# Weight loads of 512 columns, four gates at the start of tile 0, and a reordered head in an attention and SwiGLU kernel

## The chip, the cores and the metric

The kernel runs on one core of a Trainium2 chip. Its time is the device time of one execution in microseconds (us), and what is given for a kernel is the median of several executions. One further execution was recorded by the hardware profiler, and all durations below are read from that one. The engines are called as in the profile: PE (matrix products; PEld are its weight loads), DVE, ACT, POOL and SP. POOL and SP appear here almost only as the engines that issue DMA transfers.

## The reference

Attention over 4 batches of 8 heads, 768 positions and 64 channels, with 8 global keys, a causal window of 96 and a distance bias, and after it a gated feed-forward block on 3072 tokens of width 512 (hidden width 1536):

```python
scores = scale * (q @ k.T)                                  # scale = 1/8
keep = (key < 8) | ((query - key >= 0) & (query - key < 96))
dist = where(global and not local, 96, abs(query - key))
a = softmax(where(keep, scores - slope[head] * dist, -1e9))
x = (a @ v) laid out as [3072 tokens, 512]
g = x @ w_gate
out = (g * sigmoid(g) * (x @ w_val)) @ w_out
```

## The kernel before

The 3072 tokens are cut into eight tiles of 384, two for each batch (its halves). The hidden width is cut into twelve blocks f of 128. For each tile t and block f, PE makes a gate and a value (`products`, line 538): four matmuls each, one for every 128 of the 512 input channels c, from the weights `wg` and `wv` and the tile's transposed input `xT`. ACT takes a tanh of the gate (`th`, line 558), DVE makes `sl` from it and the gate (line 560), and DVE multiplies value and `sl` into `hT` (line 564). `out_part` (line 568) adds three blocks of the output product (`ops`, weights `wo`) at a time, four parts for 128 tokens.

Attention lies between these products, written by hand into the order. The heads go in pairs hp = 0 to 3. Batch 0 is done in halves. For a half of a pair, `turn_half` (line 293) transposes keys and queries on PE (`trs`), `copy_half` (line 303) copies them out of PSUM into `kT` and `qT`, `bias` (line 334) writes the distance bias into two PSUM banks by matmuls with `slopeI` and `dist`, `scores_half` (line 345) adds the key and query products to it and issues the exponentials on ACT (line 361). `Quad` then sums two pairs: denominators (`den`) and numerators (`num`), and DVE scales the numerators into `xT` (a transpose on line 449, a reciprocal, a transpose on line 455, two products on line 497).

The order in time around the change is as follows. At the start 16 fill matmuls on constants run on PE (`fill`, line 609) while the first keys and queries of pair 0 come in as float32 over SP (`k32`, `q32`) and are cast on DVE and ACT (lines 632 and 633). The other loads go over POOL's queue, which casts on the way; eight semaphores go round among them, so an issue waits until the eighth one before it has landed. The head (lines 628 to 675) makes half 0 of batch 0. Then gates and values of blocks 0 and 1 of tile 0 are made in channel order as `xT` comes in (lines 677 to 682), and the table `half1` (line 762) puts half 1 of batch 0 between the blocks of tile 0: `trh` is the transposes of two pairs, `sch` the biases and scores of one pair, `va` the denominators and numerators of two pairs. `stretches` (line 769) lists tiles, blocks and how many output parts follow each block; for tile 1 its blocks 0 to 3 have 1, 0, 1, 0 parts.

PSUM has eight banks here: a0 to a3, which `bank()` gives out in turn; x0 to x2, which `spare()` gives out in turn (from block 9 on and up to block 2 of tile 1, seven banks go round there); and o0, for outputs and for the fill matmuls. In the head the banks are named one by one.

The weights are loaded by `load_w` (line 209) for a range of blocks: for each half of the channels one transfer of `wg` and one of `wv`, cast from float32 to float16. It is called for blocks 0 to 1, 2 to 3, 4 to 7 and 8 to 11, with the loads of half 1's keys and queries (`load_half(1, ...)`) and of the values of attention (`load_v_rest`) between them; then come `wo` in four quarters and the next batch. The values of the global keys (`vG32`) come in over SP, are cast into `vG` on ACT (line 635), and two SP transfers copy them to where the numerators read them (`copy_globals(0)` on line 636, and line 637 into `vCut`).

Of the kernel before, what the change touches and what calls it, by code (L numbers as in the profile page):

```python
# [37 lines left out]
def kernel(  # L38
# [12 lines left out]
    nc = tc.nc  # L51
# [157 lines left out]
    def load_w(f0, f1):  # L209
        a, z = 128 * f0, 128 * f1  # L210
        for g in range(2):
            for w, src in ((wg, moe_w_gate), (wv, moe_w_val)):
                nc.gpsimd.dma_start(  # L213
                    out=w[:, 2 * g:2 * g + 2, a:z],
                    in_=src[256 * g:256 * g + 256, a:z].rearrange("(p s) f -> p s f", s=2))
# [46 lines left out]
    class Pair:  # L262
        def __init__(self, b, hp):
            self.b, self.hp = b, hp
            self.at = {}

# [26 lines left out]
        def turn_half(self, half, tr):  # L293
            hp = self.hp
            trq, trk = tr
            for st, dst in ((k16, trk), (q16, trq)):
# [6 lines left out]
        def copy_half(self, half, tr, k_eng, q_eng):  # L303
            trq, trk = tr
# [21 lines left out]
            else:  # L326
                part(3, 4, cut * J2, KC, 0)
                part(4, 6, 0, KC, pc - cut)
                part(6, 7, 0, S - 6 * KC, 3 * pc - cut)
            q_eng(  # L330
# [221 lines left out]
    def gate_or_val(t, f, which, c0=0):  # L552
# [3 lines left out]
        if which == 0:  # L556
            th = sb2.tile([128, TB], FP32, name="th", tag="th")
            nc.scalar.activation(out=th, in_=dst[:, 0:TB], func=AF.Tanh, scale=0.5)  # L558
            sl = sb2.tile([128, TB], FP32, name="sl", tag="sl")
            nc.vector.scalar_tensor_tensor(  # L560
                out=sl, in0=th, scalar=1.0, in1=dst[:, 0:TB], op0=AluOp.add, op1=AluOp.mult)
            gv["sl"] = sl
        else:
            nc.vector.tensor_mul(hTs[t][:, f, :], dst[:, 0:TB], gv["sl"])  # L564
# [50 lines left out]
    def p_bias(hp, which, *tags):  # L615
        pairs[0, hp].sc = pairs[0, hp].bias(0, which, [single("sc", t) for t in tags])

    def p_sc(hp, which, *tags):
        if tags:
            p_bias(hp, which, *tags)  # L620
        pairs[0, hp].scores_half(0, which, pairs[0, hp].sc)

    def p_tr(hp, kt, qt, q_eng):
        tr = [single("trs", t, FP16)[:, 0:TB] for t in (qt, kt)]
# [4 lines left out]
    fill(16)  # L629
    for h in range(4):  # L630
        make_slope(nc.scalar.mul, h)
    A(out=q16[:, 0, 0:2], in_=q32)
    V(out=k16[:, 0, 0:2], in_=k32)
    p_tr(0, "x0", "x1", A)
    A(out=vG[:, 0], in_=vG32)
    copy_globals(0)
    nc.sync.dma_start(out=vCut[0:NG], in_=vG[:, 0])
    for h in range(4, 8):
        make_slope(nc.vector.tensor_scalar_mul, h)
    load_w(0, 2)  # L640
    load_half(1, 0, 4)
    load_w(2, 4)
    load_half(1, 4, 8)
    load_w(4, 8)
    for c in range(3, NCH):
        load_v_rest(0, c)
    load_w(8, 12)
# [10 lines left out]
    p_bias(0, 0, "a0", "a1")  # L658
    p_tr(1, "x2", "o0", V)
    p_sc(0, 0)  # L660
    p_sc(0, 1, "a2", "a3")
    p_sc(1, 0, "x0", "x1")
    p_tr(2, "a0", "a1", V)
    p_sc(1, 1, "x2", "o0")
    p_tr(3, "a2", "a3", A)
    p_sc(2, 0, "a0", "a1")
    quads[0, 0].denominators(single("den", "x0"))
    p_sc(2, 1, "a2", "a3")
    p_sc(3, 0, "a0", "a1")
    for side, tag in enumerate(("x1", "x2")):  # L670
        quads[0, 0].numerators(side, single("num", tag))
    p_sc(3, 1, "a2", "a3")
    quads[0, 1].denominators(single("den", "o0"))
    for side, tag in enumerate(("x0", "x1")):
# [209 lines left out]
```

## Time and profile before

| what | value |
|---|---|
| median of 6 runs | 244.03 us (243.04 to 244.69) |
| the profiled execution's own time | 243.98 us |
| its span, first to last instruction | 242.2 us |
| matmuls of gates on line 547 | 376, 0.327 us each as drawn |
| matmuls of outputs on line 576 | 276, 0.379 us each as drawn |
| tanh of a gate, ACT, line 558 | 94, 0.496 us each |
| `sl`, DVE, line 560 | 94, 0.551 us each |
| POOL issue of a weight load, line 213 | 16, 0.71 us each |
| `wg` loads of 128 KB, issue to landing | 4, median 4.9 us |
| `wg` loads of 256 KB, issue to landing | 4, median 7.7 us |
| `wo` loads of 384 KB, issue to landing | 4, median 10.4 us |
| granted TensorE clock, whole span | 1.000 |

The span is shorter than the execution's time by 1.8 us, which lies around it. A row of the timeline gives start, length, engine, line, operation, what it writes and reads, and how many of it are merged; in brackets stands the idle time of the engine before it and what ended it. Matmuls are drawn from issue to end, and follow each other more closely than their drawn length: the distance of starts is what one costs. The chain of work that ended last is followed back from the last instruction: at each step to what released it. A row of the windows view gives a stretch, its length, the busy time of PE, PEld, DVE, ACT and POOL with counts of instructions, the granted clock, and the share and rate of the DMA engines.

### The profile page before, as it was taken

How to read it: one execution, taken by the hardware profiler on the slowest of the kernel's cores; microseconds unless marked ns; L12 is line 12 of the kernel's file. 1: busy time of each engine (PE TensorE's matmuls, PEld its weight loads, DVE VectorE, ACT ScalarE, POOL GpSimd, SP SyncE). 2: the span in 40 equal slices, each digit the busy share in tenths (PEclk: the TensorE clock that was granted, in tenths of full speed). 3: DMA queues.
4: the chain of work that ended last, by engine and by line, in shares of the span. 5: the costliest groups of instructions: out<-in, count | busy, mean ns of one | idle time of the engine just before them, and what ended most of it. 6: DMA issues, size and time to landing. Idle time of an engine off the chain costs nothing.

```text
span 242.2 us, 6053 instructions
## 1 busy us (share of the span) xinstructions
PE 235.0 (97%) x2428; PEld 135.5 (56%) x2428; DVE 166.1 (69%) x355; ACT 129.1 (53%) x294; POOL 96.6 (40%) x117
## 2 busy tenths in 40 slices
PE   7899899999999999999999999999999999999994
PEld 4455466566565556555565556555565556555543
DVE  5675749878797768767786658767786558655530
ACT  5738476787864564365455474375355535233311
POOL 8898664664990000997053242900030223000000
PEclk9999999999999999999999999999999999999999
DMA  7999999999999736899219849960110110111022
GB/s 149 172 179 196 180 206 204 196 186 131 136 137 102 161 80 123 87 121 150 50 46 96 102 129 151 101 80 1 43 46 3 43 43 3 46 43 45 0 89 87
DMA packets 84612, 25.10 MB, mean 104 GB/s; under 512 B 72816, under 2 KB 81640, under 8 KB 84584
## 3 DMA queue, kind: packets, MB, share of 16 engines
q0 software_dynamic: 65296, 14.05, 66.7%
q1 hardware_dynamic: 18856, 10.39, 17.6%
q8 instruction: 19, 0.31, 0.5%
q10 hardware_dynamic: 432, 0.27, 0.4%
q14 instruction: 9, 0.07, 0.1%
HBM read 28.67 MB, written 6.29 MB: 144 GB/s over the span
## 4 chain that ended last, share of the span: by engine, by line
PE 78%; DMA 14%; POOL 5%; ACT 1%; issue 1%; POOLq 0%
PE ops L576 24%; PE gps L547 23%; PE vps L547 22%; DMA wv<-in_moe_w_val_dram 7%; DMA wo<-in_moe_w_out_dram 5%; PE sc L379 3%; PE num L439 3%; DMA vS<-in_v_dram 3%; PE den L439 2%; PE trs L273 1%; POOL q L119 1%; POOL wg L213 1%; PE ops L592 1%; POOL k L119 1%; POOL wv L213 1%
## 5 line engine op out<-in xcount | busy, mean ns | idle before, releaser
L560 DVE SCALAR_TENSOR_TENSOR sl<-th,gps 128x384 f32<-128x384 f32 x94 | 51.8, 551 | 39.7 <-ACT th L558 38.9
L558 ACT ACTIVATE th<-gps 128x384 f32<-128x384 f32 x94 | 46.6, 496 | 59.7 <-PE gps L547 54.6
L547 PE MATMUL gps<-xT,wg 128*128 128x384 f16 x376 | 77.0, 327 | 0.5 <-DMA wg<-in_moe_w_gate_dram 0.5
L547 PE MATMUL vps<-xT,wv 128*128 128x384 f16 x376 | 76.6, 326 | 0.6 <-DMA wv<-in_moe_w_val_dram 0.6
L576 PE MATMUL ops<-wo,hT 128*128 128x512 f16 x276 | 73.3, 379 | 0.2 <-DMA wo<-in_moe_w_out_dram 0.2
L564 DVE TENSOR_TENSOR hT<-vps,sl 128x384 f16<-128x384 f32 x94 | 52.1, 554 | 8.7 <-PE gps L547 0.5
L547 PEld LDWEIGHTS <-wg 128*128 128x128 f16 x384 | 35.0, 98 | 31.8 <-issue 1.6
L547 PEld LDWEIGHTS <-wv 128*128 128x128 f16 x384 | 37.4, 98 | 26.8 <-DMA wv<-in_moe_w_val_dram 1.0
L576 PEld LDWEIGHTS <-hT 128*128 128x128 f16 x276 | 26.9, 98 | 23.9 <-issue 0.4
L387 ACT ACTIVATE at<-sc 128x432 f16<-128x432 f32 x72 | 33.9, 533 | 10.8 <-PE sc L379 10.8
L516 POOL TENSOR_TENSOR xT<-ns,rb 128x384 f16<-128x384 f32 x10 | 9.8, 994 | 66.5 <-DVE rb L455 55.6
L171 POOL DMA_DIRECT2D vS<-in_v_dram x28 | 24.7, 898 | 4.2 <-DMA kst<-in_k_dram 1.7
L582 ACT ACTIVATE osb<-ops 128x512 f32<-128x512 f32 x23 | 13.7, 597 | 14.2 <-PE ops L576 14.1
L398 POOL TENSOR_TENSOR at<-at,masks 128x864 f16<-128x864 f16 x4 | 7.3, 1821 | 23.9 <-ACT at L387 19.3
L398 DVE TENSOR_TENSOR at<-at,masks 128x864 f16<-128x864 f16 x20 | 12.2, 608 | 5.3 <-ACT at L387 5.3
L194 POOL DMA_DIRECT2D kst<-in_k_dram x16 | 14.0, 894 | 2.4 <-DMA vS<-in_v_dram 1.2
L194 POOL DMA_DIRECT2D qst<-in_q_dram x16 | 13.8, 889 | 1.8 <-DMA vS<-in_v_dram 1.1
L361 ACT ACTIVATE at<-sc 128x432 f16<-128x432 f32 (+2 forms) x32 | 11.6, 446 | 4.6 <-PE sc L350 4.6
L512 ACT COPY ns<-num 128x384 f32<-128x384 f32 x20 | 8.1, 493 | 9.3 <-PE num L439 9.3
L439 PE MATMUL num<-at,vS 128*32 128x216 f16 (+6 forms) x560 | 11.0, 226 | 0.0
L395 DVE TENSOR_TENSOR at<-at,masks 128x432 f16<-128x432 f16 x24 | 8.1, 376 | 4.0 <-ACT at L387 4.0
L449 DVE STREAM_TRANSPOSE dT<-den 128x384 f32<-128x384 f32 x16 | 9.3, 581 | 1.6 <-PE den L439 1.1
(74 smaller groups left out, 179.4 us busy)
## 6 DMA issues: line engine op xcount, KB each, us to landing
out_dram<-osb SPq DMA_DIRECT2D x23, 256.0 KB
vS<-in_v_dram POOLq DMA_DIRECT2D x24, 120.0 KB, 5.7
wo<-in_moe_w_out_dram POOLq DMA_DIRECT2D x4, 384.0 KB, 10.4
qst<-in_q_dram POOLq DMA_DIRECT2D x16, 96.0 KB, 4.4
kst<-in_k_dram POOLq DMA_DIRECT2D x16, 90.0 KB, 4.8
wg<-in_moe_w_gate_dram POOLq DMA_DIRECT2D x4, 256.0 KB, 7.7
wv<-in_moe_w_val_dram POOLq DMA_DIRECT2D x4, 256.0 KB, 8.2
kst<-in_k_dram POOLq DMA_DIRECT2D x2, 384.0 KB, 11.7
```

Source lines behind the costliest of these rows:

```text
L171: nc.gpsimd.dma_start(out=vSs[b][NG:NG + n, c, :, :], in_=v[b, :, KC * c:KC * c + n, :].rearrange("h p d -> p h d"))
L194: nc.gpsimd.dma_start(out=st[b][p0:p0 + n, h // 2, :, h % 2, :], in_=src[b, h, 0:n * J].rearrange("(t p) d -> p t d", p=n))
L361: nc.scalar.activation(out=at[:, hi, 0:col + n], in_=sc[hi][:, 0:col + n], func=AF.Exp, scale=scale)
L387: nc.scalar.activation(out=at[:, hi, :], in_=sc[hi][:, 0:BANK], func=AF.Exp, scale=scale)
L398: mul_eng.tensor_mul(at, at, m[:, :, o:o + BANK])
L439: nc.tensor.matmul(dst[r, o:o + n], lhsT=ones[:, 0:32] if side is None else vals[:, 4 * g + j, side::2], rhs=pairs[b, 2 * g + j // 2].at[c ...
L547: nc.tensor.matmul(gv[f, which][:, 0:TB], lhsT=w[:, c, 128 * f:128 * f + 128], rhs=x_of(t)[:, c, :], start=(c == 0), stop=(c == NC - 1))
L558: nc.scalar.activation(out=th, in_=dst[:, 0:TB], func=AF.Tanh, scale=0.5)
L560: nc.vector.scalar_tensor_tensor(out=sl, in0=th, scalar=1.0, in1=dst[:, 0:TB], op0=AluOp.add, op1=AluOp.mult)
L564: nc.vector.tensor_mul(hTs[t][:, f, :], dst[:, 0:TB], gv["sl"])
L576: nc.tensor.matmul(ops, lhsT=hTs[t][:, f, 128 * i:128 * i + 128], rhs=wo[:, f, :], start=(f == 0), stop=(f == NFF - 1))
L582: nc.scalar.mul(out=osb, in_=ops, mul=0.5)
```

## The change

`load_w` now takes one of the two weights and a first block, and always loads four blocks: a transfer writes rows of 512 columns (2 KB of float32 in memory), where blocks 0 to 3 had rows of 256 columns. Gates and values are loaded one after the other: gates of blocks 0 to 3, keys and queries of half 1, values of blocks 0 to 3, keys and queries, gates and values of blocks 4 to 7, and so on. There are 12 transfers of weights, not 16.

In the head, 12 fill matmuls run, not 16. Pair 0's biases stand between its key and its query transposes; its query cast is shared by ACT and DVE; the `vG` cast goes from ACT to DVE, behind pair 1's key copies; pair 1's query copy goes from DVE to ACT. Pair 1's transposes stand ahead of pair 0's scores, in the old and in the new order. Pair 1's biases follow pair 0's scores at once, the transposes of pairs 2 and 3 follow each other, and the first denominators come behind the first scores of pair 3.

Tile 0 opens with four gates (`first_gates`, in banks a0 to a3), with the transposes `trh(0, 1)` between their channels 0 to 1 and 2 to 3. The values of these blocks follow one by one between score steps (the list `tile0`), and their `sl` tiles have four buffers. Blocks 4 and 5 make both gates ahead of their values. `trh` copies keys on DVE for all pairs (ACT did it for pairs 0 and 1). In tile 1, blocks 0 to 3 have 1, 0, 0, 1 output parts.

```diff
@@ -206,13 +206,13 @@
     wg = sb.tile([128, NC, DFF], FP16, name="wg")
     wv = sb.tile([128, NC, DFF], FP16, name="wv")
     wo = sb.tile([128, NFF, DM], FP16, name="wo")
-    def load_w(f0, f1):
-        a, z = 128 * f0, 128 * f1
+    def load_w(w, f0):
+        a, z = 128 * f0, 128 * f0 + 512
+        src = moe_w_gate if w is wg else moe_w_val
         for g in range(2):
-            for w, src in ((wg, moe_w_gate), (wv, moe_w_val)):
-                nc.gpsimd.dma_start(
-                    out=w[:, 2 * g:2 * g + 2, a:z],
-                    in_=src[256 * g:256 * g + 256, a:z].rearrange("(p s) f -> p s f", s=2))
+            nc.gpsimd.dma_start(
+                out=w[:, 2 * g:2 * g + 2, a:z],
+                in_=src[256 * g:256 * g + 256, a:z].rearrange("(p s) f -> p s f", s=2))
 
     def load_wo(g):
         nc.gpsimd.dma_start(
@@ -263,6 +263,7 @@
         def __init__(self, b, hp):
             self.b, self.hp = b, hp
             self.at = {}
+            self.sc = {}
 
         def transposes(self):
             b, hp = self.b, self.hp
@@ -290,10 +291,10 @@
                 in_=k3[:, 0, NG:2 * NG].unsqueeze(1).broadcast_to([128, NCH, NG]))
 
 
-        def turn_half(self, half, tr):
+        def turn_half(self, half, tr, which=(0, 1)):
             hp = self.hp
             trq, trk = tr
-            for st, dst in ((k16, trk), (q16, trq)):
+            for st, dst in [((k16, trk), (q16, trq))[i] for i in which]:
                 for j in range(J2):
                     for hi in range(2):
                         nc.tensor.transpose(
@@ -301,6 +302,10 @@
                             st[:, half, 2 * hp + hi, D * j:D * j + D], ident)
 
         def copy_half(self, half, tr, k_eng, q_eng):
+            self.copy_keys(half, tr, k_eng)
+            self.copy_queries(half, tr, q_eng)
+
+        def copy_keys(self, half, tr, k_eng):
             trq, trk = tr
             hp = self.hp
             if half == 0:
@@ -327,6 +332,9 @@
                 part(3, 4, cut * J2, KC, 0)
                 part(4, 6, 0, KC, pc - cut)
                 part(6, 7, 0, S - 6 * KC, 3 * pc - cut)
+
+        def copy_queries(self, half, tr, q_eng):
+            trq, trk = tr
             q_eng(
                 out=self.qT[:, TB * half:TB * half + TB].rearrange("r (p j) -> r p j", j=J2),
                 in_=trq.rearrange("r (j p) -> r p j", j=J2))
@@ -556,12 +564,15 @@
         if which == 0:
             th = sb2.tile([128, TB], FP32, name="th", tag="th")
             nc.scalar.activation(out=th, in_=dst[:, 0:TB], func=AF.Tanh, scale=0.5)
-            sl = sb2.tile([128, TB], FP32, name="sl", tag="sl")
+            if t == 0 and f < 4:
+                sl = sb2.tile([128, TB], FP32, name="sl", tag="ns", bufs=4)
+            else:
+                sl = sb2.tile([128, TB], FP32, name="sl", tag="sl")
             nc.vector.scalar_tensor_tensor(
                 out=sl, in0=th, scalar=1.0, in1=dst[:, 0:TB], op0=AluOp.add, op1=AluOp.mult)
-            gv["sl"] = sl
+            gv["sl", f] = sl
         else:
-            nc.vector.tensor_mul(hTs[t][:, f, :], dst[:, 0:TB], gv["sl"])
+            nc.vector.tensor_mul(hTs[t][:, f, :], dst[:, 0:TB], gv.pop(("sl", f)))
 
     ops_t = {}
 
@@ -613,38 +624,51 @@
                              start=True, stop=True)
 
     def p_bias(hp, which, *tags):
-        pairs[0, hp].sc = pairs[0, hp].bias(0, which, [single("sc", t) for t in tags])
+        pairs[0, hp].sc[which] = pairs[0, hp].bias(0, which, [single("sc", t) for t in tags])
 
     def p_sc(hp, which, *tags):
         if tags:
             p_bias(hp, which, *tags)
-        pairs[0, hp].scores_half(0, which, pairs[0, hp].sc)
+        pairs[0, hp].scores_half(0, which, pairs[0, hp].sc[which])
+
+    def p_turn(hp, kt, qt):
+        return [single("trs", t, FP16)[:, 0:TB] for t in (qt, kt)]
 
     def p_tr(hp, kt, qt, q_eng):
-        tr = [single("trs", t, FP16)[:, 0:TB] for t in (qt, kt)]
+        tr = p_turn(hp, kt, qt)
         pairs[0, hp].turn_half(0, tr)
         pairs[0, hp].copy_half(0, tr, V, q_eng)
 
     V, A = nc.vector.tensor_copy, nc.scalar.copy
-    fill(16)
+    fill(12)
     for h in range(4):
         make_slope(nc.scalar.mul, h)
-    A(out=q16[:, 0, 0:2], in_=q32)
     V(out=k16[:, 0, 0:2], in_=k32)
-    p_tr(0, "x0", "x1", A)
-    A(out=vG[:, 0], in_=vG32)
+    tr0 = p_turn(0, "x0", "x1")
+    pairs[0, 0].turn_half(0, tr0, (0,))
+    pairs[0, 0].copy_keys(0, tr0, V)
+    A(out=q16[:, 0, 0], in_=q32[:, 0])
+    V(out=q16[:, 0, 1], in_=q32[:, 1])
+    p_bias(0, 0, "a0", "a1")
+    p_bias(0, 1, "a2", "a3")
+    pairs[0, 0].turn_half(0, tr0, (1,))
+    pairs[0, 0].copy_queries(0, tr0, A)
+    for h in range(4, 8):
+        make_slope(nc.vector.tensor_scalar_mul, h)
+    p_tr(1, "x2", "o0", A)
+    V(out=vG[:, 0], in_=vG32)
     copy_globals(0)
     nc.sync.dma_start(out=vCut[0:NG], in_=vG[:, 0])
-    for h in range(4, 8):
-        make_slope(nc.vector.tensor_scalar_mul, h)
-    load_w(0, 2)
+    load_w(wg, 0)
     load_half(1, 0, 4)
-    load_w(2, 4)
+    load_w(wv, 0)
     load_half(1, 4, 8)
-    load_w(4, 8)
+    load_w(wg, 4)
+    load_w(wv, 4)
     for c in range(3, NCH):
         load_v_rest(0, c)
-    load_w(8, 12)
+    load_w(wg, 8)
+    load_w(wv, 8)
     load_wo(0)
     load_wo(1)
     load_wo(2)
@@ -655,33 +679,33 @@
     load_qk(1, 4, 8)
     for c in range(NCH):
         load_v_rest(1, c)
-    p_bias(0, 0, "a0", "a1")
-    p_tr(1, "x2", "o0", V)
     p_sc(0, 0)
-    p_sc(0, 1, "a2", "a3")
-    p_sc(1, 0, "x0", "x1")
+    p_sc(0, 1)
+    p_bias(1, 0, "x0", "x1")
+    p_bias(1, 1, "x2", "o0")
+    p_sc(1, 0)
+    p_sc(1, 1)
     p_tr(2, "a0", "a1", V)
-    p_sc(1, 1, "x2", "o0")
     p_tr(3, "a2", "a3", A)
-    p_sc(2, 0, "a0", "a1")
-    quads[0, 0].denominators(single("den", "x0"))
-    p_sc(2, 1, "a2", "a3")
-    p_sc(3, 0, "a0", "a1")
-    for side, tag in enumerate(("x1", "x2")):
+    p_sc(2, 0, "x0", "x1")
+    p_bias(2, 1, "a0", "a1")
+    p_bias(3, 0, "a2", "a3")
+    p_sc(2, 1)
+    p_sc(3, 0)
+    quads[0, 0].denominators(single("den", "x2"))
+    p_sc(3, 1, "x0", "x1")
+    for side, tag in enumerate(("a0", "a1")):
         quads[0, 0].numerators(side, single("num", tag))
-    p_sc(3, 1, "a2", "a3")
     quads[0, 1].denominators(single("den", "o0"))
-    for side, tag in enumerate(("x0", "x1")):
+    for side, tag in enumerate(("x2", "x0")):
         quads[0, 1].numerators(side, single("num", tag))
 
-    head = [(0, 0), (0, 1), (1, 0), (1, 1)]
-    hb = [banks("gvps"), banks("gvps")]
-    for c0, c1, f0, f1 in ((0, 2, 0, 2), (2, 3, 0, 1), (3, 4, 0, 1), (2, 4, 1, 2)):
-        for f, which in head:
-            if f0 <= f < f1:
-                products(0, f, which, c0, c1, hb[f][which])
-
-
+    gv["n"] = 1
+    hb = [bank("gps") for _ in range(4)]
+
+    def first_gates(c0, c1):
+        for f in range(4):
+            products(0, f, 0, c0, c1, hb[f])
 
     def sc(b, *units):
         def step():
@@ -708,16 +732,15 @@
     def tr(b, hp):
         return pairs[b, hp].transposes
 
-    def trh(h0, h1, by_engine):
+    def trh(h0, h1, last):
         def step():
             b0, b1 = single("trs", "o0", FP16), spare("trs", FP16)
             (a, b), (c, d) = [(t[:, 0:TB], t[:, TB:2 * TB]) for t in (b0, b1)]
-            k_eng, last = (V, V) if by_engine else (A, A)
-            pair_of = [(h0, (c, a)), (h1, (d, b))] if by_engine else [(h0, (b, a)), (h1, (d, c))]
+            pair_of = [(h0, (c, a)), (h1, (d, b))]
             for hp, tr in pair_of:
                 pairs[0, hp].turn_half(1, tr)
             for hp, tr in pair_of:
-                pairs[0, hp].copy_half(1, tr, k_eng, A if hp == h0 else last)
+                pairs[0, hp].copy_half(1, tr, V, A if hp == h0 else last)
         return step
 
     def sch(hp):
@@ -759,16 +782,20 @@
         return {(t, 0): [sc(b, (0, 2), (1, 2))], (t, 3): [sc(b, (2, 2), (3, 2))],
                 (t, 7): [vas(b, 1)]}
 
-    half1 = {(0, 1): [trh(0, 1, False)], (0, 2): [sch(0)],
-             (0, 3): [sch(1), trh(2, 3, True)], (0, 5): [sch(2)], (0, 6): [sch(3)],
-             (0, 7): [va(0, 0, 1)], (0, 8): [va(0, 1, 1)]}
+    first_gates(0, 2)
+    trh(0, 1, A)()
+    first_gates(2, 3)
+    first_gates(3, 4)
+    tile0 = [(0, 0), (1, 0), (2, 0), (3, 0), (0, 1), (1, 1), sch(0),
+             (2, 1), (3, 1), sch(1), trh(2, 3, V), (4, 0), (5, 0), sch(2), (4, 1), (5, 1),
+             (6, 0), (6, 1), sch(3), (7, 0), (7, 1), va(0, 0, 1), (8, 0), (8, 1), va(0, 1, 1)]
 
     def ff(t, f0, f1, n_out=(0,)):
         return [(t, f, n_out[(f - f0) % len(n_out)]) for f in range(f0, f1)]
 
     stretches = [
-        (ff(0, 0, 10) + ff(0, 10, 12, (1,)), half1),
-        (ff(1, 0, 4, (1, 0)) + ff(1, 4, 10, (1,)) + ff(1, 10, 12, (2,)), first(1, 1)),
+        (ff(0, 9, 10) + ff(0, 10, 12, (1,)), {}),
+        (ff(1, 0, 4, (1, 0, 0, 1)) + ff(1, 4, 10, (1,)) + ff(1, 10, 12, (2,)), first(1, 1)),
         (ff(2, 0, 12, (1,)) + ff(3, 0, 12, (1,)), both(2, 1)),
         (ff(4, 0, 12, (1,)) + ff(5, 0, 12, (1,)), both(4, 2)),
         (ff(6, 0, 12, (1,)), second(6, 3)),
@@ -821,6 +848,16 @@
         for step in step_list:
             step()
 
+    for item in tile0:
+        if callable(item):
+            take([item])
+            continue
+        f, which = item
+        run_later(1)
+        gate_or_val(0, f, which, NC if f < 4 and which == 0 else 0)
+        for fn in after.pop((0, f, which), []):
+            fn()
+
     for tiles, steps in stretches:
         for t, f, n_out in tiles:
             for ld in loads.pop((t, f), []):
@@ -830,7 +867,7 @@
                     run_later(1)
             for which in range(2):
                 run_later(1)
-                gate_or_val(t, f, which, NC if t == 0 and f < 2 else 0)
+                gate_or_val(t, f, which)
                 for fn in after.pop((t, f, which), []):
                     fn()
             for n in range(n_out):
```

## The prediction

> **What bounds the kernel now.** I read first the busy table, then the chain of work that ended last over the first 50 us, then the PE timeline around the chain's DMA pieces, then the DMA rate in windows of one microsecond.
>
> ```profile
> PE 235.0 (97%) x2428; PEld 135.5 (56%) x2428; DVE 166.1 (69%) x355; ACT 129.1 (53%) x294; POOL 96.6 (40%) x117
> ```
>
> TensorE is busy 97% of the span, so time can only be won where PE waits. The windows view gives PE 44.87 of 45 us busy from 55 to 100, and 50.00 of 50 in both stretches from 100 to 200: there nothing is to be had. What is left lies before 50 us, and there the chain is not PE at all (start, length, what):
>
> ```profile
> 19.23 8.49 DMA wv<-in_moe_w_val_dram
> 27.73 0.29 issue
> 28.02 7.86 DMA wv<-in_moe_w_val_dram
> 35.88 0.28 issue
> 36.16 11.73 DMA wo<-in_moe_w_out_dram
> 47.89 0.04 issue
> 47.93 0.81 PE ops L576 x3
> ```
>
> Up to 47.93 us the chain is POOL's queue of loads, each issue waiting for the landing of the eighth before it. PE meets it in two places:
>
> ```profile
> 25.32 0.50 PE L547 MATMUL gps<-xT,wg 128*128 128x384 f16 x2
> 26.34 0.50 PE L547 MATMUL gps<-xT,wg 128*128 128x384 f16 x2 [0.53 <-DMA wg<-in_moe_w_gate_dram]
> 26.68 0.49 PE L547 MATMUL vps<-xT,wv 128*128 128x384 f16 x2
> 27.77 0.50 PE L547 MATMUL vps<-xT,wv 128*128 128x384 f16 x2 [0.60 <-DMA wv<-in_moe_w_val_dram]
> 28.11 0.33 PE L547 MATMUL gps<-xT,wg 128*128 128x384 f16 x1
> ...
> 46.91 0.81 PE L547 MATMUL vps<-xT,wv 128*128 128x384 f16 x4
> 47.93 0.81 PE L576 MATMUL ops<-wo,hT 128*128 128x512 f16 x3 [0.21 <-DMA wo<-in_moe_w_out_dram]
> ```
>
> The bracket understates a wait, since a matmul's drawn end overlaps the next start. Undisturbed, a gate and a value of four matmuls start 0.65 apart. From 25.32 to 28.11 is 2.79 for one pair that should take 1.30: **1.49 us lost** at block 4. From 46.91 to 47.93 is 1.02 instead of 0.65: **0.37 lost** at wo's last quarter. Between them PE runs without a gap, but value 8 starts at 36.01 just after its weights landed (28.02 + 7.86 = 35.88). So whoever removes the first stall meets the DMA queue again there.
>
> **The change, part by part.**
>
> *Rows of 2 KB.* Gate and value weights of blocks 0 to 3 now come as four loads, not eight: 1.05 MB in rows of 1024 B in SBUF, not 512 B. The queue never pauses here, so a byte's rate is the price. One-microsecond windows (length, busy times, granted clock, DMA share, GB/s), the first two with 512 B rows, the others with 1024 B rows:
>
> ```profile
> 16.00:17.00 1.00, 1.00 (x7) 0.49 (x5) 0.90 (x2) 0.00 (x0) 1.00 (x2) 1.00 1.33 171
> 18.00:19.00 1.00, 1.00 (x12) 0.49 (x12) 0.36 (x1) 0.89 (x2) 1.00 (x2) 1.00 1.41 176
> 22.00:23.00 1.00, 1.00 (x12) 0.59 (x9) 0.81 (x2) 0.97 (x4) 1.00 (x2) 1.00 1.25 207
> 24.00:25.00 1.00, 1.00 (x30) 0.80 (x30) 0.90 (x2) 0.56 (x3) 0.73 (x1) 1.00 1.24 205
> ```
>
> 1.05 MB take 6.06 us at 173 GB/s and 5.11 at 205: every later load lands **0.95 us earlier**. Bounds: nothing, if the rate there was set by something else; four POOL issues of 0.71 = 2.8 us, if issuing set it. I take 0.95, from the rows for the same loads.
>
> The Trainium skill, "DMA: Bandwidth & Descriptors", section Specifications, speaks against this: it asks for at least 512 B per transfer for line rate, which the old rows already have. By that rule this part saves nothing and the total would be 243.2; by the rows it is 242.2. The measured 173 against 205 differs from the rule, so I go by the rows.
>
> *Head, up to the first gates.* PE runs four fill matmuls fewer (0.213 each, 0.85), so pair 0's key transposes start when k16 is cast (3.55 + 0.36) instead of at 4.64. That gain is hidden: pair 1's keys land at 6.34 and PE waits for them today ("0.41 <-DMA k" before 6.38). The diff leaves pair 1's transposes ahead of pair 0's scores, so these still start near 7.15. Casting q half on ACT, half on DVE puts DVE's half behind three key copies (4.5 + 0.66, then about 0.26): query transposes at 5.5 instead of 5.14, hidden by the same wait. Pair 0's two biases (0.39 + 0.27) fill that gap; only the second is new there and 0.27 leaves the later path. Then pairs 2 and 3 transpose before pair 2's bias, and pair 2's queries land at 9.38 in both versions. From there, following PSUM banks and ACT's exps (0.43 and 0.19 each), I get the last scores 0.8 us earlier but the first denominators at 12.1 instead of 11.38, since they now stand behind pair 3's first scores. DVE's chain from there (transpose, reciprocal, transpose, two products: 2.58 us from 15.12 to 17.70 today, and run twice) ends at about 17.8, as today. **No gain, no loss**, with PE doing half-1 transposes (0.79) while it waits.
>
> *The vG cast on DVE.* It moves from ACT (5.92) behind pair 1's key copies, to about 7.45 to 7.9. SP's two copies queue behind it. Today they issue at 6.55 and 7.47 and their landing marks stand at 12.17 and 12.57; issued at 7.9 and 8.8 they land at 13.5 and 13.9, where numerators would like to start at 13.0. PE waits 0.6 to 0.9 for them. It is mostly absorbed by the DVE chain: four gates and the transposes are done at 18.85, against 19.61 today for the same PE work (two gates, two values, transposes).
>
> *Four gates first.* They hold banks a0 to a3 until four tanh (0.49 each on ACT, behind two query copies) and four DVE products (0.55). The first half-1 scores need all four banks: a3 comes free at about 21.25, PE wants it at 20.6. **0.6 us new wait**, between nothing (ACT done early) and 1.5 (DVE's six key copies, 1.28 on line 316, take longer). Scores end at 22.0; today at 22.11 with the same number of products done.
>
> *Block 4 and on.* Now the price list: gate and value 1.30, scores 1.09 (21.02 to 22.11), transposes 0.79, values of attention 1.02. From 22.0: values 2, 3 at 23.3; scores 24.4; transposes 25.2; gates 4, 5 at 26.5 (their weights are now issued ahead of the values' and land near 24); scores 27.6; values 4, 5 at 28.9 (landing 27.73 - 0.95 = 26.8); block 6, scores, block 7, attention to 33.6; gate 8 to 34.3; half of value 8 to 34.6. **The 1.49 stall goes.** Next late is wv's last load: 35.88 - 0.95 = 34.93. PE waits 0.3, does its last two products by 35.26; today value 8 ends at 36.66. **Gain 1.40.**
>
> *wo's last quarter.* The outputs of part 3 move from block (1,2) to (1,3), behind four transposes (1.46) and one pair (1.30). It lands at 47.89 - 0.95 = 46.9 and is wanted at about 48.8: **the 0.37 goes too**. The transposes ahead of it need qst (issue 32.70 + 12.81 = 45.5, less 0.95), wanted at 46.3: 1.7 of margin.
>
> Sum: 1.40 + 0.37 = 1.77. After 50 us the same PE work runs gapless. The profiled execution took 243.98 us (span 242.2 plus 1.8 around it), the median of the runs is 244.03; 243.98 - 1.77 = **242.2**.
>
> **Rivals.**
> 1. *2 KB rows bring no speed.* For it: other queues share the windows at 173. Against it: four windows agree. wv lands at 35.88, value 8 ends 36.21: gain 0.45 + 0.37, **243.2**.
> 2. *The new waits are longer.* vG's copies a microsecond later, or banks held 1.5: PE reaches value 8 late, and beyond 0.3 us each microsecond costs one. Lateness of 1.2 to 1.8: **243.1 to 243.7**.
> 3. *Slower: TensorE stays at half rate.* The granted clock reads 1.00 everywhere, yet the fill matmuls start 0.213 apart for 256 columns (1.2 per ns), and 384 columns take 0.163 at 15.9 (2.4 per ns). The pace doubles at about 4.5 us, after 3.3 us of fill. With 12 fills PE pauses 0.2 at 3.7 and waits again near 5.2 and 6.0. If the pace doubles only at 7.8, the wait for q at 9.38 hides it. If not before 17.7, about 8.3 us of stream get half done: 4.1 late, value 8 ends at 39.0, loss 2.4 less 0.37, **246.0**. It decides once PE is 2.1 us late, that is with half rate to about 13.6. Against it: transposes and biases go on, and today's similar pauses (5.8, 8.8) don't lower the pace.
> 4. *PE arrives early or the queue gains more than 0.95* (issuing counted): value 8 unhindered, about **241.6**.
>
> The Trainium skill, "TensorE: Matmul & The Clock Gate", Part 1: The HAM clock gate, has half rate until about 3.4 us of sustained activity, in a window that doesn't start with the kernel. Twelve fills are 2.6 us, so by that rule rival 3's first step could happen; how busy a window must be, no row shows.
>
> **How the numbers follow.** Forecast 0.52; rival 4 0.08; rival 1 0.17; rival 2 0.15; rival 3 0.08. This kernel's measurement tells about 0.3% (0.73 us) from no change, so faster means below 243.30. Forecast and rival 4 are faster, half of rivals 1 and 2 too: 0.76. The rest of these is within it, 0.16; rival 3 is slower, 0.08. The range runs from 241.5 (rival 4) to 243.8 (rival 2's end), and leaves out rival 3 and some of the edges.
>
> **What would show it.** Right: no idle before block 4's products; the chain still on POOL's loads until wv, landing near 34.9; PE waiting there a few tenths; no idle before the outputs on line 576; windows with the first weight loads near 205 GB/s. Wrong: wv's last landing still at 35.9 (rival 1); score biases waiting for DVE's sl, or numerators for vS, by over a microsecond (rival 2); transposes and biases at 0.1 us per 128 columns after 9.4 (rival 3); or new PE idle after 50 us, which I exclude.

## The result and the profile after

The changed kernel took **242.44 us** (median of 21 runs, 242.04 to 245.76) against 244.06 us for the kernel before on the same chip (42 runs): ratio **0.9939**, 95% interval 0.9925 to 0.9953, so 1.5 us faster by the ratio and 1.6 by the medians. Its profiled execution took 242.93 us with a span of 241.2 us; that of before took 243.98 us with 242.2. The forecast was 242.2. In some executions the granted clock of TensorE falls to half for 3.41 us or a multiple of it; executions with about one such stretch (a mean clock of 0.991 to 0.993) are dearer by 0.5 to 2.1 us in the medians of the kernels below. So beside the ratio stands the median of the executions whose mean granted clock was at least 0.998, called "at full clock": 242.44 for the changed kernel. For the kernel before it is 243.72, 243.71 and 243.78 in the three sets of executions beside the experiments; those of the first comparison have no clock on record.

The busy table of the changed kernel, and the chain by engine:

```profile
PE 233.4 (97%) x2424; PEld 135.4 (56%) x2424; DVE 166.8 (69%) x362; ACT 127.7 (53%) x288; POOL 93.9 (39%) x113
PE 90%; POOL 4%; DMA 3%; ACT 1%; DVE 1%; issue 0%; ACTq 0%; POOLq 0%
```

The shares of the engines hardly moved, but the chain did: DMA's part of it was 14% and is 3%, PE's was 78% and is 90%. The chain (start, length, what; its longest pieces) shows where the queue of loads lets go:

```profile
9.98 7.79 DMA q<-in_q_dram
17.81 0.69 PE trs L300 x18
18.50 0.93 PE gps L555 x5
19.46 0.50 ACT th L566
19.98 0.56 DVE sl L571
20.64 0.50 ACT th L566
21.16 1.03 DVE sl L571 x2
22.57 0.41 PE sc L358 x10
22.98 1.41 PE vps L555 x8
```

Before, POOL's loads set the end until 47.93 us; now they do so only until half 1's queries land at 17.77. Then come the tanh and `sl` of the first gates, which hold the banks that the first half-1 scores want, and from 22.57 on PE without a break. PE's timeline (start, length, engine, line, operation; in brackets the idle time before it and what ended it):

```profile
15.04 1.53 PE L555 MATMUL gps<-xT,wg 128*128 128x384 f16 x8
16.80 0.36 PE L300 MATMUL trs<-ident,k 128*64 128x128 f16 x6 [0.23 <-DMA k<-in_k_dram]
17.81 0.36 PE L300 MATMUL trs<-ident,q 128*64 128x128 f16 x6 [0.65 <-DMA q<-in_q_dram]
...
18.44 1.48 PE L555 MATMUL gps<-xT,wg 128*128 128x384 f16 x8
19.75 0.49 PE L555 MATMUL vps<-xT,wv 128*128 128x384 f16 x2
20.42 1.15 PE L555 MATMUL vps<-xT,wv 128*128 128x384 f16 x6 [0.18 <-DMA wv<-in_moe_w_val_dram]
21.41 1.17 PE L347 MATMUL sc<-dist,slopeI 128*128 128x72 f16 x6
...
26.11 1.47 PE L555 MATMUL gps<-xT,wg 128*128 128x384 f16 x8
27.43 0.76 PE L347 MATMUL sc<-dist,slopeI 128*128 128x72 f16 x6
```

Three things are to be seen. Blocks 4 and 5 (26.11 on) have no bracket: the 1.49 us stall is gone. The four gates are done at 19.75, where their first value starts. The biases at 21.41 take 1.17 us where the next ones take 0.76: a bank wait of 0.4 us that the merged row hides. The first value also waits, for `wv`: its third matmul starts at 20.42, 0.34 later than in an undisturbed row. And the same view further on:

```profile
35.33 0.81 PE L555 MATMUL vps<-xT,wv 128*128 128x384 f16 x4
...
49.10 0.81 PE L555 MATMUL vps<-xT,wv 128*128 128x384 f16 x4
49.75 0.81 PE L587 MATMUL ops<-wo,hT 128*128 128x512 f16 x3
50.40 0.81 PE L555 MATMUL gps<-xT,wg 128*128 128x384 f16 x4
```

The first and the last of these rows stood so in the kernel before:

```profile
36.01 0.81 PE L547 MATMUL vps<-xT,wv 128*128 128x384 f16 x4
...
51.45 0.81 PE L547 MATMUL gps<-xT,wg 128*128 128x384 f16 x4
```

Value 8 starts at 35.33 (before 36.01): 0.68 us earlier. The outputs at 49.75 have no wait, where those of before had 0.37. The gate at 50.40 is that of block 4 of tile 1; the same PE work stands ahead of it in both orders, and before it started at 51.45. So 0.68 + 0.37 = 1.05 us were won by 50 us, and that is what the two profiled executions differ by, 243.98 - 242.93. After 50 us nothing more was won or lost.

### The profile page after: what moved, and what is told of

It reads as the page before. It is cut to its first block, busy times and chain, and to the rows that moved or that the text cites. A ratio compares the mean times of both kernels' runs of the same rounds, so it can differ in the third digit from the quotient of the medians.

```text
span 241.2 us, 6040 instructions
## 1 busy us (share of the span) xinstructions
PE 233.4 (97%) x2424; PEld 135.4 (56%) x2424; DVE 166.8 (69%) x362; ACT 127.7 (53%) x288; POOL 93.9 (39%) x113
## 4 chain that ended last, share of the span: by engine, by line
PE 90%; POOL 4%; DMA 3%; ACT 1%; DVE 1%; issue 0%; ACTq 0%; POOLq 0%
PE gps L555 26%; PE vps L555 25%; PE ops L587 24%; PE sc L387 3%; PE num L447 3%; DMA q<-in_q_dram 3%; PE den L447 2%; PE trs L274 1%; POOL vS L171 1%; PE ops L603 1%; POOL k L119 1%; PE sc L347 1%; PE sc L358 1%; DVE sl L571 1%; ACT th L566 1%; PE trs L300 1%
## 5 line engine op out<-in xcount | busy, mean ns | idle before, releaser
L566 ACT ACTIVATE th<-gps 128x384 f32<-128x384 f32 x96 | 47.4, 495 | 58.8 <-PE gps L555 53.2
L571 DVE SCALAR_TENSOR_TENSOR sl<-th,gps 128x384 f32<-128x384 f32 x96 | 52.7, 551 | 37.3 <-ACT th L566 36.6
L555 PE MATMUL vps<-xT,wv 128*128 128x384 f16 x384 | 77.8, 326 | 0.2 <-DMA wv<-in_moe_w_val_dram 0.2
L555 PE MATMUL gps<-xT,wg 128*128 128x384 f16 x384 | 77.9, 327 | 0.0
L575 DVE TENSOR_TENSOR hT<-vps,sl 128x384 f16<-128x384 f32 x96 | 53.1, 554 | 9.6 <-PE vps L555 1.3
```

The costliest lines, as they stand in the source:

```text
L555: nc.tensor.matmul(gv[f, which][:, 0:TB], lhsT=w[:, c, 128 * f:128 * f + 128], rhs=x_of(t)[:, c, :], start=(c == 0), stop=(c == NC - 1))
L571: nc.vector.scalar_tensor_tensor(out=sl, in0=th, scalar=1.0, in1=dst[:, 0:TB], op0=AluOp.add, op1=AluOp.mult)
L575: nc.vector.tensor_mul(hTs[t][:, f, :], dst[:, 0:TB], gv.pop(("sl", f)))
```

## Experiments

All kernels are variants of the changed kernel, unless it says otherwise; the ratio is to the kernel before on the same chip. My theory from the two profiles: the gain needs the order of the loads, the order of tile 0 and the place of the outputs together, and the head is worth nothing. The rivals: the rows' speed alone does it, or the outputs' place alone, or the head.

**The head alone taken back.** The 16 fills, whole query cast on ACT, `vG` cast on ACT and the old order of scores, ahead of the new loads and tile 0:

```diff
-    fill(12)
+    fill(16)
...
+    A(out=vG[:, 0], in_=vG32)
...
-    V(out=vG[:, 0], in_=vG32)
...
-    p_sc(0, 1)
-    p_bias(1, 0, "x0", "x1")
-    p_bias(1, 1, "x2", "o0")
-    p_sc(1, 0)
-    p_sc(1, 1)
+    p_sc(0, 1, "a2", "a3")
+    p_sc(1, 0, "x0", "x1")
```

> The changed kernel with the old head (16 fill matmuls, the old order of transposes, biases and scores, vG cast on ACT). My theory: the head is hidden by the loads, as the prediction said; the changed kernel stands at 242.44, and this one comes out at 242.2 to 242.8. Rival (the head's order made the gain): 243.2 to 244.0.

Measured 242.37 us, ratio 0.9945 (0.9923 to 0.9968). In the medians the head is worth nothing, as the prediction had it (the changed kernel took 242.44 and, in a later run, 242.72). PE's timeline in this kernel:

```profile
18.78 1.61 PE L555 MATMUL vps<-xT,wv 128*128 128x384 f16 x8
20.22 0.39 PE L347 MATMUL sc<-dist,slopeI 128*128 128x72 f16 x4
20.79 0.81 PE L347 MATMUL sc<-dist,slopeI 128*128 128x432 f16 x2 [0.18 <-DVE sl L571]
...
34.36 0.93 PE L555 MATMUL vps<-xT,wv 128*128 128x384 f16 x4
```

The four gates are done at 18.78 here, a microsecond earlier than in the changed kernel. Value 8 starts at 34.36 and its third matmul waits for the last load of `wv`, which lands at 34.75 (it starts at 34.79, 0.1 us late).

**The old loads.** The changed order of products with rows of 256 columns, gate and value interleaved:

```diff
-    load_w(wg, 0)
+    load_w(0, 2)
     load_half(1, 0, 4)
-    load_w(wv, 0)
+    load_w(2, 4)
     load_half(1, 4, 8)
-    load_w(wg, 4)
-    load_w(wv, 4)
+    load_w(4, 8)
```

> The changed kernel with the old loads of weights (16 transfers, gate and value in turn, rows of 256 columns for blocks 0 to 3, old places in POOL's queue). My theory: the order of the loads must fit the order of the products; the four first gates then wait for wg of blocks 2 and 3, which landed at 19.98 in the kernel before, some 2 us later than wg now, and part of it comes back: 243.0 to 243.8. Rival (the head or the order of products on PE made the gain, whatever the loads): 242.2 to 242.8.

Measured 244.6 us, ratio 1.0042 (1.0013 to 1.0072); at full clock 243.99 against 243.72 before. The gain is gone. The timeline names the wait, which ends before the granted clock falls to half in this execution (19.11):

```profile
18.74 1.14 PE L555 MATMUL gps<-xT,wg 128*128 128x384 f16 x4 [2.08 <-DMA wg<-in_moe_w_gate_dram]
```

Four gates at the start want the gate weights of blocks 2 and 3, which come after two value loads and half 1's first loads here.

**The old tile 0.** The new loads and head, with two gates and two values at the start, the table `half1` and outputs as before:

```diff
-    first_gates(0, 2)
-    trh(0, 1, A)()
-    first_gates(2, 3)
-    first_gates(3, 4)
...
+    half1 = {(0, 1): [trh(0, 1, False)], (0, 2): [sch(0)],
...
-        (ff(1, 0, 4, (1, 0, 0, 1)) + ff(1, 4, 10, (1,)) + ff(1, 10, 12, (2,)), first(1, 1)),
+        (ff(1, 0, 4, (1, 0)) + ff(1, 4, 10, (1,)) + ff(1, 10, 12, (2,)), first(1, 1)),
```

> The kernel before with the new loads and the new head, but the old order of tile 0 (gate and value of each block in turn, two blocks in channel order) and the old places of the outputs in tile 1. My theory: the gain needs PE's order and the loads' order together; the second product then waits for wv of blocks 0 to 3 (19.0 to 20.4 in the profile after), 3 us later than today: 244.3 to 246.0, no faster than before. Rival (wider rows alone gain 0.95 us, as the prediction had it): 242.9 to 243.4.

Measured 245.06 us, ratio 1.0046 (1.002 to 1.0072); at full clock 244.35, so 0.6 slower than before. Loads with all gates first, under an order that wants values early, are worse than both kernels with this head. How the 0.6 us come about is not shown: the profiled execution (248.23 us) has half rate from 14.56 to 24.80, and in it the second product waits 0.72 us for `wv`, as expected, but ahead of it the numerators wait 1.52 and 1.78 us for the new head's `vG` copies.

**Narrow rows in the new order.** Only the row length is taken back, and with it the number of transfers (eight for blocks 0 to 3, not four):

```diff
-        a, z = 128 * f0, 128 * f0 + 512
...
+        step = 256 if f0 == 0 else 512
         for g in range(2):
...
+            for a in range(128 * f0, 128 * f0 + 512, step):
+                z = a + step
...
```

> The changed kernel, with the four loads of blocks 0 to 3 cut into eight of 256 columns each, in the same order and places. Prediction's step (1.05 MB at 173 instead of 205 GB/s): later loads land 0.95 us later and value 8 with them, 243.2 to 243.5. My theory after seeing the profile (the last landing mark of each load moved only by 0.07 to 0.36 us, because one lagging DMA engine sets it): 242.5 to 242.9.

Measured 243.27 us, ratio 0.9972 (0.9948 to 0.9997); at full clock 242.87. Against the changed kernel's two medians (242.44, and 242.72 in a later run) the rows are worth 0.2 to 0.4 us at full clock and 0.6 to 0.8 over all executions, a third of which have half rate here. Value 8 waits for its weights, which land at 35.98, and loses 0.40 by the starts (line 557 here is line 555 of the changed kernel):

```profile
36.03 0.50 PE L557 MATMUL vps<-xT,wv 128*128 128x384 f16 x2 [0.24 <-DMA wv<-in_moe_w_val_dram]
```

**The outputs' place alone,** in the kernel before, and **taken back,** in the changed kernel:

```diff
-        (ff(1, 0, 4, (1, 0)) + ff(1, 4, 10, (1,)) + ff(1, 10, 12, (2,)), first(1, 1)),
+        (ff(1, 0, 4, (1, 0, 0, 1)) + ff(1, 4, 10, (1,)) + ff(1, 10, 12, (2,)), first(1, 1)),
```

> The kernel before, with only the outputs of tile 1's blocks 0 to 3 in the new places (1, 0, 0, 1 instead of 1, 0, 1, 0). My theory: the 0.37 us that PE waits for wo's last quarter goes and nothing else changes: 243.35 against 243.72 for the kernel before. Rival (PE meets the same landing somewhere else): 243.6 to 243.8.

> The changed kernel with the outputs of tile 1 back in their old places. My theory: wo's last quarter is waited for again, by 0.4 us or a little more, as PE now comes earlier and the load hardly does: 242.8 to 243.1 against 242.43. Rival (the wait was hidden): 242.4.

Alone it gave 243.6 us, ratio 0.9987 (0.9973 to 1.0002), at full clock 243.51: 0.2 us, which the interval doesn't tell from nothing. Taken back it cost more than forecast: 243.47, ratio 0.998 (0.9961 to 0.9999), at full clock 243.38, 0.7 to 0.9 above the two medians of the changed kernel. Its own profile doesn't show why. That execution (244.28 us) has half rate from 14.82 to 18.23, PE comes late, `wo`'s last quarter landed at 47.04, and there is no wait:

```profile
47.56 0.81 PE L555 MATMUL vps<-xT,wv 128*128 128x384 f16 x4
48.20 0.81 PE L587 MATMUL ops<-wo,hT 128*128 128x512 f16 x3
```

In the changed kernel's profile, the old place would want that quarter at 46.89, where the value that starts at 46.24 ends. In the eight profiles of the changed order with these loads it landed at 46.91 to 47.62. From these numbers I estimate a wait of 0 to 0.7 us; whether this is what was lost stays open.

**Half 1's transposes behind all four gates,** so that they don't wait for the queries:

```diff
     first_gates(0, 2)
-    trh(0, 1, A)()
     first_gates(2, 3)
     first_gates(3, 4)
+    trh(0, 1, A)()
```

> The changed kernel, with the half-1 transposes of pairs 0 and 1 behind all four gates, not between their channels. My theory: PE no longer stands for the queries of half 1 (in the profile after it waited 0.8 us for them at 17.81), but value 8 then waits for wv's last load, so little is won: 242.2 to 242.5 against 242.43. Rival (PE's order in tile 0 is the limit, not the load): 241.6 to 242.0.

Measured 244.35 us, ratio 1.0021 (1.0 to 1.0043); at full clock 243.88, 1.2 to 1.4 worse than the changed kernel's two medians. Both expectations missed, since neither looked at DVE:

```profile
21.75 0.28 PE L347 MATMUL sc<-dist,slopeI 128*128 128x72 f16 x2 [0.53 <-DVE sl L571]
22.21 0.28 PE L347 MATMUL sc<-dist,slopeI 128*128 128x72 f16 x2 [0.19 <-DVE sl L571]
22.86 0.81 PE L347 MATMUL sc<-dist,slopeI 128*128 128x432 f16 x2 [0.37 <-DVE sl L571]
```

The six key copies now stand ahead of the `sl` products on DVE, and the biases wait for the banks three times, 1.09 us together by the brackets. By the starts, biases and scores of this step take 2.96 us, where the next ones take 1.10: 1.9 us lost, against 0.4 in the changed kernel. The first value starts at 19.74, as in the changed kernel (19.75), and value 8 at 36.42, 1.09 later, without a wait for its weights. So the whole loss lies between the two.

**More slack for the loads** (old head; half 1's first loads between the two gate loads; both attention steps ahead of block 8):

```diff
-    load_w(wg, 0)
+    load_w(wg, 0, (0,))
     load_half(1, 0, 4)
+    load_w(wg, 0, (1,))
...
-             (6, 0), (6, 1), sch(3), (7, 0), (7, 1), va(0, 0, 1), (8, 0), (8, 1), va(0, 1, 1)]
+             (6, 0), (6, 1), sch(3), (7, 0), (7, 1), va(0, 0, 1), va(0, 1, 1), (8, 0), (8, 1)]
```

> The changed kernel with the old head; keys and queries of half 1 are loaded between the two halves of the first gate weights, and block 8 comes behind both attention sums instead of between them. My theory: value 8 then comes 1.0 us later in PE's order and never meets wv's last load, and the half-1 transposes find their data: 241.9 to 242.2 against 242.37 with the old head. Rival (another load becomes the one that is waited for, such as wo's first quarter or wv of blocks 0 to 3): 242.3 to 242.7.

Measured 243.78 us, ratio 0.9996 (0.998 to 1.0012). The gain is gone, and mostly not to a load: the second attention's numerators wait 0.80 us for DVE (`dT`) and value 9 waits 0.33 for `sl`. The first value waits 0.62 for `wv`, which here comes behind half 1's first loads.

```profile
34.93 0.79 PE L447 MATMUL num<-at,vS 128*32 128x72 f16 x40 [0.80 <-DVE dT L457]
...
38.10 0.81 PE L555 MATMUL vps<-xT,wv 128*128 128x384 f16 x4 [0.33 <-DVE sl L571]
```

**The changed kernel again, with the `vG` cast back on ACT, with 16 fills, and a combination.** The first three were run to see whether the late copies of `vG` and the half clock reach the end. The fourth has the old head, a buffer of its own for each of the first four tanh, and half of value 8 behind the second attention step.

```diff
     pairs[0, 0].copy_queries(0, tr0, A)
+    A(out=vG[:, 0], in_=vG32)
+    copy_globals(0)
+    nc.sync.dma_start(out=vCut[0:NG], in_=vG[:, 0])
...
-    V(out=vG[:, 0], in_=vG32)
-    copy_globals(0)
-    nc.sync.dma_start(out=vCut[0:NG], in_=vG[:, 0])
```

```diff
-    fill(12)
+    fill(16)
```

```diff
-            th = sb2.tile([128, TB], FP32, name="th", tag="th")
+            if t == 0 and f < 4:
+                th = sl = sb2.tile([128, TB], FP32, name="sl", tag="ns", bufs=4)
...
-             (6, 0), (6, 1), sch(3), (7, 0), (7, 1), va(0, 0, 1), (8, 0), (8, 1), va(0, 1, 1)]
+             (6, 0), (6, 1), sch(3), (7, 0), (7, 1), va(0, 0, 1), (8, 0), va(0, 1, 1), (8, 1)]
```

> The changed kernel once more, beside the next three on the same chip. If its time is what the first look gave: 242.4. If TensorE's drop to half rate, seen in the granted clock of several kernels with the new head (3.41 us long, about 1.2 us dearer), is drawn by chance at each execution, some executions of this one lie at 243.5 to 244.5 and the median of the rest stays at 242.4. If the first look was lucky, the median is 243.5 or more.

> The changed kernel with the vG cast back on ACT, ahead of pair 1's transposes, so SP's two copies issue about 1 us earlier. Theory A (this wait is absorbed by the DVE chain and by the wait for pair 0's half-1 queries): the same as the changed kernel within 0.2, 242.4. Theory B (the numerators' wait of 0.45 us, 1.45 in one profile, reaches the end): 242.0. Theory C (the pause there is what lets the granted clock fall to half): fewer executions with a half-rate stretch, the undisturbed ones as in A.

> The changed kernel with 16 fill matmuls in place of 12 (0.85 us more of fill). Theory A (the head is hidden by the landings of k and q and by the DVE chain): the same within 0.2, 242.4, and full rate begins earlier than the 5.0 us of the changed kernel. Theory B (the head is on the path): 243.2. Theory C (four fewer fills are what leaves TensorE prone to the half-rate stretch): fewer executions with one.

> The changed kernel with the old head, with each of the first four gates' tanh in a buffer of its own (sl is computed in its place) and with the second half of value 8 behind pair 1's attention values. Theory A (score biases wait for the tanh buffers, and value 8 for the last weights of wv; both are on the path): 0.2 to 0.5 less than the old head's 242.37, so 241.9 to 242.2. Theory B (the last weights and wo's quarter set the end whatever PE does before): 242.3 to 242.4. Theory C (the second attention's numerators then wait for DVE, as in the run that had both ahead of block 8): 242.5 to 243.

The changed kernel gave 242.72 us, ratio 0.9951 (0.9936 to 0.9967): 1.1 to 1.2 us of gain here, 1.5 in the first comparison (1.3 at full clock, against 243.72); none of its six executions had half rate. With the cast on ACT it gave 242.55, ratio 0.9947 (0.9932 to 0.9962): the same within 0.2, so most of the copies' lateness is absorbed. The timeline of the repeat, and then that of the kernel with the cast on ACT:

```profile
14.71 0.43 PE L447 MATMUL num<-at,vS 128*32 128x216 f16 x12 [0.99 <-DMA vS<-vG]
21.70 0.81 PE L347 MATMUL sc<-dist,slopeI 128*128 128x432 f16 x2 [0.33 <-DVE sl L571]
```

```profile
12.70 0.43 PE L447 MATMUL num<-at,vS 128*32 128x216 f16 x12 [0.46 <-ACT at L369]
...
16.80 0.36 PE L300 MATMUL trs<-ident,q 128*64 128x128 f16 x6 [0.51 <-DMA q<-in_q_dram]
17.43 1.48 PE L555 MATMUL gps<-xT,wg 128*128 128x384 f16 x8
18.74 0.49 PE L555 MATMUL vps<-xT,wv 128*128 128x384 f16 x2
20.32 1.15 PE L555 MATMUL vps<-xT,wv 128*128 128x384 f16 x6 [1.08 <-DMA wv<-in_moe_w_val_dram]
```

The numerators start 2 us earlier, the four gates are done a microsecond earlier (18.74 against 19.69), and then the first values wait 1.08 us for `wv`: more than half of that microsecond is given back, and value 8 starts 0.45 earlier (34.82 against 35.27). With 16 fills the time was 244.22, ratio 1.0009 (0.9986 to 1.0033); only 4 of 12 executions were at full clock, with 242.86. Theory C, which expected fewer with half rate, met the opposite. The combination gave 243.18, ratio 0.997 (0.9955 to 0.9985), slower than the old head alone. Its time is nearest to theory C, but the wait is another one: the numerators don't wait, and the gate of block 10 waits for a bank that DVE holds with value 8's product (group `hT`), queued behind the second attention's chain:

```profile
38.41 0.81 PE L555 MATMUL gps<-xT,wg 128*128 128x384 f16 x4 [0.69 <-DVE hT L575]
```

No variant's ratio is below 0.9939, the changed kernel's in the first comparison.

## Why the prediction was right, and where its sizes were off

**Block 4's stall and wo's wait: right.** Both are gone. Of the 1.86 us that they cost together, the profiled execution has 1.05 as gain.

**Rows of 2 KB, 0.95: about right at the landing.** The last load of `wv` landed at 35.88, 35.47, 35.98 and 36.32 with narrow rows (before, outputs alone, narrow rows in the new order, old loads), mean 35.91. With wide rows and this list of loads it landed at 35.52, 34.75, 36.18, 35.16, 35.01, 34.81, 34.96, 35.62 and 35.51 (changed kernel, old head, old tile 0, later transposes, outputs back, repeat, cast on ACT, 16 fills, combination), mean 35.28: 0.63 us earlier. A load lands with its last of 16 marks, and that one can come late by itself (last section); by the 13th mark the means are 35.32 and 34.42, 0.9 apart. The windows that showed 171 and 176 GB/s before (last number of a row) show in the changed kernel:

```profile
16.00:17.00 1.00, 0.77 (x10) 0.32 (x8) 0.89 (x2) 0.00 (x0) 0.50 (x1) 1.00 1.26 201
18.00:19.00 1.00, 1.00 (x22) 0.71 (x19) 0.62 (x4) 0.45 (x2) 0.71 (x1) 1.00 1.51 192
```

With narrow rows in the new order they show 175 and 189. So rival 1 falls: for these casting loads, rows of 1024 B in SBUF moved faster than rows of 512 B, although the Trainium skill ("DMA: Bandwidth & Descriptors", Specifications) has line rate from 512 B on. Whether the row in SBUF, the row in memory (2 KB against 1 KB) or the number of transfers makes the difference, these runs don't separate. What of it reaches the time is less, 0.2 to 0.8: in the changed kernel's two profiles PE comes to value 8 late by itself (35.33 and 35.27) and doesn't wait for these weights.

**The head, nothing: right in the medians** (242.37 with the old head). The first denominators came at 12.12, as worked out (12.1).

**The new bank wait, 0.6: right.** Biases and scores of this step take 1.50, 1.87 and 1.72 us by the starts in the changed kernel, its repeat and the old head, where the next ones take 1.09: 0.4, 0.8 and 0.6 lost. The chain names its cause as forecast (`th` and `sl` of the first gates), and the experiment with later transposes shows its price when DVE comes later still.

**The step that was mis-sized is "four gates and the transposes are done at 18.85", and with it the term 1.40.** They were done at 19.75, value 8 came 0.68 us earlier than before and not 1.40, and the limit there wasn't "wv's last load": in the repeat it landed at 34.81 and PE came at 35.27 by itself. Two causes are seen, one in each profile of the changed kernel. In the first, the queries of half 1 landed at 17.77: 15 of the load's 16 landing marks stood by 16.64, and the last came 1.1 us later. Behind the gates the first value then lost 0.34 us to `wv` (1.25 with the cast on ACT), a wait that isn't in the prediction at all. In the repeat the queries were there, but the numerators waited 0.99 for the `vG` copies, which left SP at 8.18 where I had 7.9. Where neither happened, with the old head, the gates were done at 18.78 and the same working holds to the end: the gate of block 4 of tile 1 started at 49.54, 1.91 us earlier than before, against 1.77 forecast. But that was the fastest of nine executions; their median, 242.37, is close to the changed kernel's. So the medians at full clock give a gain of 1.1 to 1.3, and what holds back the other 0.5 to 0.7 in the usual execution is seen only in these single profiles, and is not settled. That the forecast of 242.2 and the 242.44 lie so near is partly luck: the other median of the changed kernel is 242.72.

**The outputs, 0.37: right in the profile, low in the experiments** (0.2 alone, 0.7 to 0.9 taken back). That a PE which comes earlier to the last quarter of `wo` has more to lose there would fit, but no profile shows it.

**Rival 2** came in part: single waits for the `vG` copies are 0.45 to 1.78 us long in the profiles with the cast on DVE, and moving it back to ACT won 0.2 us at most in the medians. **Rival 3** was not the usual case, but its mechanism is real, in another place than I put it. In the repeat, half rate lasted to 9.85 us in the profiled execution (transposes 0.107 apart for 128 columns until then, 0.056 after), and it still took 242.87, 0.15 above that run's median: half rate up to there costs little, as worked out. What I excluded, that "similar pauses" lower the clock later, is what the next section shows.

## What to carry to other kernels

Before changing an order to remove a stall, list what the next limit is in the queue of loads, in the buffers and on the second engine, and change them together: here loads, products and outputs were worth 1.1 to 1.5 us together, and of these the outputs alone 0.2, the new loads without the new tile 0 or the new tile 0 without the new loads a loss. In three variants that took a wait for a load away, a few instructions on DVE became the next limit. And a pause of PE early in a kernel should be priced twice, once as a wait and once as a risk for its clock.

## What the runs showed of the hardware

**The granted clock goes by a grid of 3.41 us.** In five of the fourteen profiles the clock, once full, falls to half within the first 25 us. These half-rate stretches were 3.41, 6.83 or 10.24 us long, and the full-rate stretches ahead of them 3.41, 10.24 or 13.65. The grid doesn't start with the kernel: the first full-rate window began at 4.50 us before, 5.02 in the changed kernel and 9.85 in its repeat. Windows view of the kernel with 16 fills, cut by that grid (length, busy times, granted clock, DMA share, GB/s):

```profile
7.98:11.39 3.41, 3.27 (x52) 1.88 (x52) 1.93 (x8) 3.37 (x11) 3.40 (x5) 1.00 2.12 162
11.39:14.81 3.42, 1.69 (x45) 1.05 (x44) 1.39 (x3) 2.04 (x7) 2.90 (x4) 1.00 1.37 205
14.81:18.22 3.41, 2.24 (x69) 2.12 (x70) 1.92 (x5) 0.00 (x0) 1.51 (x3) 0.50 1.34 200
18.22:21.63 3.41, 3.41 (x24) 1.77 (x26) 1.52 (x3) 0.00 (x0) 2.50 (x3) 0.50 1.44 200
21.63:25.05 3.42, 3.35 (x34) 2.08 (x31) 2.64 (x9) 2.60 (x6) 2.27 (x3) 1.00 1.26 202
```

In 11.39 to 14.81 PE is busy 1.69 us, as it waits 1.49 and then again for `vG` copies, and the next window has half rate; that window is busy 2.24 us and half rate stays; the next is busy all through and full rate returns. Two more kernels bound the point: narrow rows (the first two rows below), then later transposes.

```profile
4.97:8.38 3.41, 2.13 (x33) 1.32 (x32) 2.23 (x12) 0.96 (x3) 3.41 (x5) 1.00 1.44 157
8.38:11.79 3.41, 3.41 (x40) 2.19 (x38) 1.82 (x7) 3.10 (x9) 2.99 (x5) 0.50 2.11 160
```

```profile
12.61:16.03 3.42, 2.19 (x84) 1.83 (x85) 2.35 (x6) 0.58 (x3) 2.59 (x4) 1.00 1.45 197
16.03:19.44 3.41, 2.75 (x32) 1.56 (x31) 1.80 (x4) 0.00 (x0) 2.37 (x3) 1.00 1.36 203
```

A window at full rate with 2.13 us of drawn busy time was followed by half rate, one with 2.19 was not. Cut by this grid, the first 30 us of the other profiles agree: full-rate windows ahead of a fall have 1.34 to 2.13 us, all others 2.19 or more. The Trainium skill ("TensorE: Matmul & The Clock Gate", Part 1: The HAM clock gate) has the same free-running window of about 3.4 us, but asks for an idle window before half rate returns; these windows were half busy.

**Where the `vG` cast stands goes with it.** Kernels with the cast on DVE issued the copies at 7.47 to 8.72 us, and 35 of their 100 executions had a mean granted clock under 0.998; those with it on ACT, the kernel before among them, issued at 6.49 to 6.99, and 8 of 141 had. It isn't shown as the cause: all but one of the latter have the old head too, and the one that doesn't had 0 of 6, where the changed kernel had 2 of 28. Why 16 fills gave 8 of 12 stays open.

**The last landing mark of a load can lag behind the others for many loads.** Each of POOL's loads leaves 16 landing marks. In the changed kernel's profile the second gate load had 15 of them by 14.55 and the last at 16.21, and for the next ten loads the last mark stayed 1.2 to 1.6 us behind the 13th; with the old head it was 0.14 behind at the queries of half 1 (16.49 and 16.63). A 16 KB instruction fetch of 0.96 us stands at 14.15 in the trace; that it is the cause was not tried.
